# First-layer gate and value weights as scaled float16 pairs in blocks 0 and 1

## The chip, the cores and the metric

The kernel runs on one core of a Trainium2 chip. The metric is the device time of one execution in microseconds (us). The engines are named as the profile names them: PE (TensorE, the matrix engine; PEld is its weight load), DVE (VectorE), ACT (ScalarE), POOL (GpSimd) and SP (SyncE, which issues nearly all DMAs, in order).

## The reference

```python
# attention: q, k, v are (4, 8, 576, 64); tau = 0.02
scores = 0.125 * q @ k.T
scores = where(scores >= max(scores) - tau, scores, -1e9)
attn = exp(scores - max); attn = attn / (sum(attn) + 1e-9);  a = attn @ v
x = a as (2304 tokens, 512)
# layer 0: w_gate, w_val (512, 1536), w_out (1536, 512)
xn = x / sqrt(mean(x*x) + 1e-6) * rms_g
g = xn @ w_gate;  y = (g * sigmoid(g) * (xn @ w_val)) @ w_out
# layer 1: the same without the norm, with weights of its own
g = y @ w_gate2;  out = (g * sigmoid(g) * (y @ w_val2)) @ w_out2
```

All arrays are float32. The kernel reaches nearly that accuracy with products of split operands: each operand is a pair (high part, rest), and a product is three matmuls (high x high, high x rest, rest x high), written `for a, b_ in ((0, 0), (0, 1), (1, 0))`.

## The kernel before

The 2304 tokens are cut into three **blocks** of 768 (`NB`, `TW`; half a block is `HT` = 384 columns). A layer over a block is 18 **units** of weights (`NU`): 12 gate-and-value units (`gate_val`, 128 columns of gate and 128 of value each; the list `GV`) and 6 output units (`outp`). Units are numbered through: 0 to 17 are block 0, layer 0; 18 to 35 block 0, layer 1; 36 to 53 block 1, layer 0; 54 to 71 block 1, layer 1; 72 to 107 block 2. A unit before 54 is 48 matmuls of 384 columns (`dense`): per 128 columns of weights four slices, three products, two halves. From unit 55 on, gate-and-value units use seven products in place of eight (`gate_val7`, `weights7`); in block 2 these run on scaled float16 pairs, elsewhere on `float32r`, the type of all products of units 0 to 53.

Attention is cut into 48 tiles per block. Those of block 0 run first, alone; those of block 1 are interleaved with block 0's units, those of block 2 with block 1's layer 0. The first two units (`NRAW`) are computed on `x * rms_g` without the token's norm (`put_raw`) and scaled afterwards; then `norm(0)` writes the normed block into `XS`, the split input of a layer. At the end of a layer's `outp(2)`, `put` writes the next layer's `XS`.

**Weights.** In block 0, each unit is loaded as 1 MB of 64-bit words and turned to float32 by three ACT steps and one of DVE (L1006 to L1009, into one of two `w32` buffers); `w_split` (L968, L970) then makes the pair: ACT copies to `float32r`, DVE (for units in the set `W_E`) or POOL subtracts. The pair lies in one of three buffers (`r_w`) and is stored to DRAM for block 1 (`kept`, 1 MB); gate-and-value units also store the float32 weights (`kept2`, 0.5 MB). Units in the set `K_E` store the float32 weights alone, and are split again in block 1. In block 1, layer 1, `square_sum` (L863, L864) reads each of layer 0's gate-and-value units back and sums its squares; `power` turns the sums to scales, powers of two, for block 2's float16 pairs. The sum for `rms_g` is spread by a matmul inside `rms(1)` (L820).

**Order.** All operations are collected with priorities (`SU`, `ST` and the offsets `OFFS`) and put into an order by a list scheduler in the file (`Program.order`), which uses costs given with each operation. Each engine then runs its instructions in that order. The sets `V_E`, `Q_E`, `X_E`, `P_E`, `T_E`, `H_E` and others choose the engine of single operations.

Of the kernel before, what the change touches and what calls it, by code (L numbers as in the profile page):

```python
# [88 lines left out]

V_E = {1, 3, 6, 7, 8, 12, 14, 15, 16, 21, 24, 27, 28, 29, 30, 31, 32, 33, 35, 36, 37, 38, 39, 40, 43, 44, 46, 47, 48, 51, 53, 55, 56, 58, 59, 61, 63, 64, 66, 67, 68, 82, 83, 87, 90, 91, 95, 96, 97, 98, 100, 101, 102, 103, 106, 107, 109, 112, 116, 117, 122, 124, 125, 127}  # L90
K_E = {1, 3, 6, 7, 8, 12, 14, 18, 19, 20, 22, 24, 25, 26, 30, 31, 32, 33, 34}
W_E = {1, 2, 3, 6, 8, 11, 12, 13, 14, 16, 17, 18, 19, 21, 25, 27, 29, 30, 31, 33, 34, 37, 40, 41, 42, 44, 46, 49, 50, 51, 52, 55, 56, 57, 58, 59, 61, 62, 63, 64, 69, 72, 73, 74, 75, 78, 81, 82, 83, 85, 87, 89, 92, 93, 94, 96, 98, 99, 100, 102, 103, 106, 108, 110, 111, 113, 114, 117, 120, 121, 122, 125, 131, 133, 137, 138, 139, 141, 143}
H_E = {0, 1, 2, 4, 5, 8, 9, 11, 12, 14, 15, 18, 20, 21, 22, 23, 25, 27, 28, 32, 33, 34, 35, 36, 37, 40, 41, 44, 45, 46, 47, 48, 49, 51, 54, 55, 56, 57, 58, 59, 60, 61, 64, 65, 68, 69, 73, 74, 80, 84, 85, 87, 88, 93, 94, 95}
X_E = {0, 2, 4, 6, 8, 12, 17, 21, 22, 25, 28, 32, 33, 34, 35, 40, 41, 42, 43, 44, 47, 48, 50, 51, 55, 57, 58, 59, 62, 63, 64, 66, 74, 77, 80, 81, 82, 83, 85, 86, 87, 88, 89, 90, 91, 92, 93, 94, 96, 98, 99}
P_E = {0, 1, 2, 3, 4, 6, 7, 10, 12, 13, 14, 15, 16, 17, 18, 19, 22, 23, 25, 28, 29, 30}
# [1323 lines left out]
```

## Time and profile before

| | us |
|---|---|
| median of 3 runs | 1143.38 (1142.97 to 1148.64) |
| profiled execution | 1145.37 |
| its span, first to last instruction | 1143.5 |
| PE busy / DVE / ACT / POOL | 1108.9 / 908.4 / 792.1 / 613.5 |

A busy PE is not a PE at its peak: a matmul's bar is longer than the distance to the next one. The speed of PE is read from the distance of starts inside a run of matmuls. The trace shows attention of block 0 up to about 131 us, the units of block 0 to about 500 us, block 1's layer 0 to about 718 us, its layer 1 to about 872 us, and block 2 to the end.

### The profile page before, as it was taken

Reading aid. Unit: us, or ns where it says so; the run is one execution under the profiler, and the core shown is the slowest. Engines: PE = TensorE matmul, PEld = TensorE weight load, DVE = VectorE, ACT = ScalarE, POOL = GpSimd, SP = SyncE. Lnnn points to the kernel's source line nnn. Section 1 sums busy time; section 2 is a strip of 40 time slices with the busy share of each in tenths; the row PEclk is TensorE's granted clock in tenths of the full one; section 3 lists DMA queues with packets and bytes.
Section 4 is the critical chain, followed back from the end, with each engine's and each line's share of the span. In section 5 each row is a group of like instructions: output and inputs, shape, how many; then the busy total and the mean of one; then the engine's idle time right before and its main releaser. Section 6 shows DMA issues by size and latency. Waiting matters only on the chain.

```text
span 1143.5 us, 19688 instructions
## 1 busy us (share of the span) xinstructions
PE 1108.9 (97%) x7106; PEld 966.6 (85%) x7106; DVE 908.4 (79%) x1642; ACT 792.1 (69%) x1175; POOL 613.5 (54%) x818
## 2 busy tenths in 40 slices
PE   8989999999999999999999999999999999999998
PEld 5656889989999999998999998999997768668677
DVE  7989598988987888887888897876479767896844
ACT  5798689878889887645866555756675766776621
POOL 5476146765678887448798874143501264224501
PEclk8999999999999999999999999999999999999999
DMA  6564349999899999957788786733755232223011
GB/s 173 182 212 154 102 144 270 269 266 309 235 260 244 262 245 251 271 159 195 164 187 181 185 187 158 256 101 133 258 181 180 72 118 92 64 104 111 19 38 56
DMA packets 178898, 201.44 MB, mean 176 GB/s; under 512 B 144368, under 2 KB 148208, under 8 KB 168816
## 3 DMA queue, kind: packets, MB, share of 16 engines
q1 hardware_dynamic: 178512, 200.18, 61.7%
q8 instruction: 56, 0.92, 0.3%
q14 instruction: 42, 0.34, 0.1%
q10 hardware_dynamic: 288, 0.00, 0.0%
HBM read 135.66 MB, written 36.18 MB: 150 GB/s over the span
## 4 chain that ended last, share of the span: by engine, by line
PE 59%; DVE 14%; DMA 10%; ACT 6%; POOL 6%; issue 4%; SPq 0%; ACTq 0%; POOLq 0%; DVEq 0%
PE ps L1076 19%; PE pt L1113 7%; PE pbPA L1113 6%; PE pbPD L1076 5%; PE pbPB L1076 5%; DMA w<-kept 4%; DMA arena<-arena 4%; PE pt L1076 3%; PE ps L719 2%; PE pt L772 2%; PE pt L675 2%; PE ps L615 2%; PE pt L654 1%; POOL arena L578 1%; ACT w L864 1%
## 5 line engine op out<-in xcount | busy, mean ns | idle before, releaser
L1076 PE MATMUL ps<-XS,w 128*128 128x384 f32 x1152 | 210.5, 339 | 3.0 <-DVE th L1195 1.4
L1076 PEld LDWEIGHTS ps<-XS,w 128*128 128x128 f32 x1152 | 199.6, 189 | 5.1 <-DVE th L1195 1.7
L1113 PEld LDWEIGHTS <-arena 128*128 128x128 f16 x1008 | 97.2, 98 | 66.7 <-issue 4.1
L1076 PE MATMUL pt<-XS,w 128*128 128x384 f32 x600 | 111.0, 337 | 3.3 <-DVE th L1179 3.0
L1076 PE MATMUL ps<-h,w 128*128 128x384 f32 x576 | 106.9, 341 | 1.7 <-DVE col L734 0.7
L1076 PEld LDWEIGHTS pt<-XS,w 128*128 128x128 f32 x600 | 102.9, 188 | 5.7 <-DVE th L1179 4.6
L1047 POOL TENSOR_TENSOR arena<-w,arena 128x384 f16<-128x384 f32 (+3 forms) x52 | 62.3, 1223 | 81.9 <-ACT arena L1045 74.5
L1076 PEld LDWEIGHTS ps<-h,w 128*128 128x128 f32 x576 | 101.4, 190 | 3.5 <-issue 1.7
L1218 POOL TENSOR_TENSOR h<-th,h 128x384 fp32r<-128x384 f32 (+1 forms) x35 | 55.3, 1592 | 91.1 <-ACT h L1214 91.0
L735 ACT ACTIVATE arena<-ps,col 128x576 f32<-128x576 f32 x96 | 70.5, 737 | 38.4 <-DVE col L734 20.6
L733 DVE TENSOR_REDUCE col<-ps 128x1 f32<-128x576 f32 x96 | 71.4, 751 | 27.0 <-PE ps L719 26.8
L736 DVE SCALAR_TENSOR_TENSOR arena<-ps,col,arena 128x576 f32<-128x576 f32 x96 | 77.5, 810 | 13.8 <-ACT arena L735 13.4
L1214 ACT CAST h<-th 128x768 fp32r<-128x768 f32 x72 | 60.0, 833 | 38.9 <-DVE th L1176 14.1
L1113 PE MATMUL pt<-rx,arena 128*128 128x384 f16 (+1 forms) x384 | 82.8, 330 | 0.8 <-ACT tq L1122 0.8
L1076 PE MATMUL pbPB<-h,w 128*128 128x384 f32 x420 | 82.2, 340 | 1.3 <-DVE h L1218 1.3
L1076 PE MATMUL pbPD<-h,w 128*128 128x384 f32 x420 | 80.8, 339 | 1.4 <-DVE h L1218 0.8
L1113 PE MATMUL pbPA<-rx,arena 128*128 128x384 f16 (+1 forms) x368 | 78.8, 330 | 2.8 <-ACT SS L1122 1.9
L578 POOL TENSOR_TENSOR arena<-arena 128x512 f16<-128x512 f32 x68 | 81.0, 1193 | 0.1
L1076 PEld LDWEIGHTS pbPD<-h,w 128*128 128x128 f32 x420 | 73.7, 188 | 2.5 <-DVE h L1218 1.2
L1076 PEld LDWEIGHTS pbPB<-h,w 128*128 128x128 f32 x420 | 73.9, 188 | 2.3 <-DVE h L1218 1.6
L559 ACT ACTIVATE arena<-arena,col 128x576 f32<-128x576 f32 x76 | 65.0, 864 | 14.6 <-DVE col L746 8.9
L1042 DVE TENSOR_TENSOR w<-w 128x256 f32<-128x256 f32 x108 | 58.1, 554 | 20.9 <-DMA w<-kept 11.5
(275 smaller groups left out, 2696.9 us busy)
## 6 DMA issues: line engine op xcount, KB each, us to landing
w<-kept SPq DMA_DIRECT2D x77, 512.0 KB, 4.0
w<-in_w SPq DMA_DIRECT2D x36, 1024.0 KB, 6.8
w<-kept SPq DMA_DIRECT2D x25, 1024.0 KB, 5.5
kept<-w SPq DMA_DIRECT2D x17, 1024.0 KB, 4.8
kept<-w SPq DMA_DIRECT2D x26, 512.0 KB, 4.1
arena<-in_qkv SPq DMA_DIRECT2D x40, 160.0 KB, 4.2
ra<-in_qkv SPq DMA_DIRECT2D x10, 576.0 KB, 4.7
out<-Y SPq DMA_DIRECT2D x11, 384.0 KB, 2.9
```

The costliest lines, as they stand in the source:

```text
L559: op("ACT", 760, lambda: nc.scalar.activation(e, e, AF.Identity, bias=c[:, 4:5], scale=c[:, 3:4]), **k)
L578: op(en, 601 if eng == 2 else 1128, lambda: n1.tensor_tensor(h[:, 640:], e[:, :512], h[:, :512], ALU.subtract), lock=True, w=[("lo", n)], ...
L615: nc.tensor.matmul(s[m:m + w, jj, :b - a], x[k, c0:c0 + w], x[k, S + a:S + b], start=True, stop=True)
L733: op("DVE", 670, lambda: nc.vector.tensor_reduce(c[:, 0:1], s2, AX.XY, ALU.max, negate=True), w=[*sk, ("mx", n)], bufs=[cb], p=T + F['MAX' ...
L735: op("ACT", 640, lambda: nc.scalar.activation(e2, s2, AF.Exp, bias=c[:, 2:3], scale=SCALE), r=[("thr", n)], w=[*sk, ("e", n)] + ek, bufs=[ ...
L736: op("DVE", 750, lambda: nc.vector.scalar_tensor_tensor(e2, s2, c[:, 1:2], e2, ALU.is_ge, ALU.mult, accum_out=c[:, 6:7]), r=[("thr", n)], ...
L1042: op(en, 345 if en == "DVE" else 740, lambda n1=n1, o=o, x=x, y=y, alu=alu: n1.tensor_tensor(q(o), q(x), q(y), alu), lock=True, w=[("w32", ...
L1047: op(en, 70 + (z - a) * 105 // 100 if en == "DVE" else 190 + (z - a) * 210 // 100, lambda a=a, z=z: n2.tensor_tensor(hv(1)[:, a:z], st[:, ...
L1076: nc.tensor.matmul(pt[:, j, :HT] if len(halves) == 2 else pt(), w(i, a), x(i, b_)[:, j * HT:(j + 1) * HT], start=(i == 0 and a == 0 and b_ ...
L1113: nc.tensor.matmul(bank(), w()[:, a, col * 256 + i * P:][:, :P], xf(i, b_), start=first and i == 0 and a == 0 and b_ == 0, stop=i == 1 and ...
L1214: op("ACT", 734, lambda: nc.scalar.copy(h[:, 0], tb.t), r=[("th", n)], w=[("h0", n)], bufs=[tb, hb], p=p, name=f"h{n}")
L1218: op(eng, 72 + (z - a) * 105 // 100 if eng == "DVE" else 190 + (z - a) * 209 // 100, lambda a=a, z=z: n1.tensor_tensor(h[:, 1, a:z], tb.t[ ...
```

## The change

Layer 0's gate-and-value units of blocks 0 and 1, but for units 0 and 1, become scaled float16 pairs, and so does their input `XS`. Units 0 and 1 stay `float32r` in block 0; their twins 36 and 37 are float16. The scales are made in block 0: after a unit's conversion, ACT sums its squares, PE spreads the sum over the partitions, and six small DVE operations make the scales; ACT and DVE then make the pair (`split16`). Tanh and value operations take the scales as operands. The pair is stored (`keptg`, 0.5 MB) with the float32 weights (`kept2`, 0.5 MB), and block 1 loads the pair as it is; units 36 and 37 are split from float32. `K_E` keeps only layer 1's units. `square_sum` in block 1, layer 1, goes. The three weight buffers become `A`, `B` and a third that is either one `float32r` buffer (`C`) or two of float16 (`D`, `E`): layer 0's float16 units take turns on D and E, its other units on A and B, layer 1's on C, A, B. `XS` changes its type with each layer (`GEN`), so a `put` waits for all reads of the old `XS`. All offsets and most of the engine sets have other values.

```diff
-K_E = {1, 3, 6, 7, 8, 12, 14, 18, 19, 20, 22, 24, 25, 26, 30, 31, 32, 33, 34}
+K_E = {18, 19, 20, 22, 24, 25, 26, 30, 31, 32, 33, 34}
...
+    GEN = (1, 2, 3, 4, 5, 5)
...
-    r_w = ring("w", 3, [P, 2, 1024], F32R)
+    WT = [sb.tile([P, 2, 1024], F32R, name=f"w{i}") for i in range(2)]
+    late["wc", 1] = sb.tile([P, 2048], F32, name="wc_3", tag="wc")
...
+    def half16(n):
+        return n < SB0 and n % (2 * NU) in GV[:NF] and n >= NRAW
+
+    def w_next(n):
+        layer = n // NU
+        g = min(layer, 3) + 1
+        cycle = "DE" if half16(n) else ("AB", "CAB")[layer % 2 or layer > 3]
...
-            if b == 1:
-                nc.tensor.matmul(bank(pk)[:, 400:401], ones[:, 0:1].to_broadcast([P, P]), SETS16[0][0][:, 12:13], start=True, stop=True)
...
+    def col_sum(x, r, p):
+        op("PE", 100, lambda: nc.tensor.matmul(PA[:, 1, 400:401], ones[:, 0:1].to_broadcast([P, P]), x, start=True, stop=True), r=r, w=["SCB"], p=p, name="scales", cols=0)
...
     def norm(b):
-        T = SU(36 * b) - 3000 + 0
+        T = SU(36 * b) - 3000 + (NP0, NP1, NP2)[b]
         last = b == NB - 1
+        xsb.ops = old()
...
-        if gen == 1:
+        if gen:
             bufs = bufs + [Buf(None, xsb)]
...
+    def split16(n, k, w, ws, b32, sbf, p):
+        sc = SETS16[0][2][:, k:k + 1]
+        op("ACT", 939, lambda: nc.scalar.activation(ws()[:, 0], w, AF.Copy, scale=sc), ...)
+        op("DVE", 1142, lambda: nc.vector.scalar_tensor_tensor(ws()[:, 1], w, sc, ws()[:, 0], ALU.mult, ALU.subtract), ...)
...
+            if half16(n):
+                if i in K_E or i < NRAW:
+                    op("DMA", 1500, lambda: nc.sync.dma_start(w, kept[i][:, 0] if i in K_E else kept2[i]), ...)
+                    split16(n, GV.index(i), w, ws, b32, sbf, T + O(n)['WS2'])
+                else:
+                    op("DMA", 1500, lambda: nc.sync.dma_start(ws(), keptg[i]), ...)
+                return
...
-        w_split(n, w, ws, b32, sbf, T + O(n)['WS'])
+        if n < NU and n in GV:
+            k = GV.index(n)
+            op("ACT", 1100, lambda: nc.scalar.activation(t.bitcast(BF16)[:, :1024], w, AF.Square, accum_out=SETS16[0][0][:, k:k + 1]), ..., name=f"wsq{n}")
+            col_sum(SETS16[0][0][:, k:k + 1], [("SSQ", 0, n)], T + O(n)['WS'] + O(n)['WR'])
+            power(0, lambda: (PA[:, 1, 400:401], 1.0), ["SCB"], k, k + 1, ...)
+            unit_scales(0, T + O(n)['WS'] + O(n)['WR'], k, k + 1)
+        if half16(n):
+            split16(n, GV.index(n), w, ws, b32, sbf, T + O(n)['WS'])
+        else:
+            w_split(n, w, ws, b32, sbf, T + O(n)['WS'])
...
+        elif n < NU and n in GV:
+            if half16(n):
+                op("DMA", 1500, lambda: nc.sync.dma_start(keptg[n], ws()), ..., name=f"keep{n}")
+            op("DMA", 1500, lambda: nc.sync.dma_start(kept2[n], w), ..., name=f"keep{n}")
...
-                dense(pt, pk, NC, ..., lambda i, a: XSF()[:, a, i], wk, xk, [wb], T, U)
+                dense(pt, pk, NC, ..., lambda i, a: XSF(xg)[:, a, i], wk, xk, [wb], T, U, ns=165 if h16 else 175)
...
-                if b == 1 and m == 1:
-                    square_sum(GV[f], SETS16[0][0][:, f:f + 1], ("SSQ", 0), T)
-                    if f == NF - 1:
-                        weight_scales(0, T)
-                        unit_scales(0, T)
```

## Rows read from the trace of the kernel before

**Rows 1.** Page, busy time: engine, us, share of the span, instructions.
```profile
PE 1108.9 (97%) x7106; PEld 966.6 (85%) x7106; DVE 908.4 (79%) x1642; ACT 792.1 (69%) x1175; POOL 613.5 (54%) x818
```
**Rows 2.** Stages: PE, PEld, DVE, ACT, POOL busy us (instructions), clock, DMA share, GB/s.
```profile
150.00:310.00 160.00, 156.87 (x938) 149.57 (x937) 139.51 (x223) 134.20 (x164) 102.84 (x121) 1.00 0.93 261
310.00:486.00 176.00, 173.70 (x1056) 162.50 (x1056) 148.41 (x240) 144.07 (x177) 131.83 (x155) 1.00 0.97 254
502.00:718.00 216.00, 211.21 (x1417) 198.08 (x1416) 177.66 (x392) 135.02 (x228) 165.02 (x254) 1.00 0.76 179
718.00:872.00 154.00, 149.18 (x849) 145.51 (x848) 112.28 (x186) 99.91 (x163) 48.51 (x39) 1.00 0.53 183
872.00:1143.50 271.50, 265.91 (x1587) 198.13 (x1585) 197.79 (x312) 159.97 (x241) 84.75 (x78) 1.00 0.23 81
```
**Rows 3.** PE's waits in 150 to 310 us: us in total, times, longest.
```profile
PE ps L1076 <- DVE th L1195: 1.6, 2, 1.4
PE ps L719 <- DVE arena L736: 0.9, 1, 0.9
```
**Rows 4.** Timeline of PE, float32r runs: start, us, line, tile, shapes, count.
```profile
263.50 8.48 PE L1076 MATMUL ps<-XS,w 128*128 128x384 f32 x48
...
293.60 7.59 PE L1076 MATMUL ps<-h,w 128*128 128x384 f32 x42
```
**Rows 5.** Timeline of PE, float16 runs of block 2.
```profile
894.66 1.14 PE L1113 MATMUL pt<-rx,arena 128*128 128x384 f16 x6
895.64 1.14 PE L1113 MATMUL pbPA<-rx,arena 128*128 128x384 f16 x6
```
**Rows 6.** Timeline of PE, one-column and two-column matmuls.
```profile
129.12 1.50 PE L818 MATMUL pt<-small,SS 128*128 128x2 f32 x12
...
485.91 0.36 PE L820 MATMUL pt<-sqs,small 128*128 128x1 f32 x2
```
**Rows 7.** Timeline of DVE, first and last of four dependent scale operations.
```profile
487.87 0.15 DVE L869 TENSOR_SCALAR sqs<-pt 128x1 f32<-128x1 f32 x1
...
488.49 0.14 DVE L872 TENSOR_SCALAR sqs<-sqs 128x1 int32<-128x1 int32 x1
```
**Rows 8.** The sums of squares: ns min/median/max, first and last start us.
```profile
L864 ACT ACTIVATE w<-w x30: 1040/1057/1074, 656.0 to 843.6; 128x1024 bf16<-128x1024 f32 x30
L864 ACT ACTIVATION_READ_ACCUMULATOR w<-w x30: 185/186/206, 657.0 to 844.5; 128x1 f32 x30
```
**Rows 9.** Groups by shape, pair's rest: busy us, mean ns, idle before.
```profile
L970 DVE TENSOR_TENSOR w<-w,w 128x1024 fp32r<-128x1024 f32 x28 | 42.4, 1516 | 4.7 <-ACT w L968 4.6
L1047 DVE TENSOR_TENSOR arena<-w,arena 128x1024 f16<-128x1024 f32 x15 | 20.3, 1353 | 0.0
```
**Rows 10.** Stage 500 to 718 us: busy us (count) of ACT at L968.
```profile
500.00:718.00 218.00, 8.37 (x8) 1.00 0.76 178
```
**Rows 11.** Timeline around the switch from unit 1 to unit 2, all engines.
```profile
141.27 4.67 PE L1076 MATMUL ps<-XS,w 128*128 128x384 f32 x26
...
144.02 3.02 ACT L952 CAST XS<-X 128x768 fp32r<-128x768 f32 x4
...
145.81 3.55 DVE L955 TENSOR_TENSOR XS<-X,XS 128x768 fp32r<-128x768 f32 x4
...
146.81 4.43 PE L1076 MATMUL ps<-XS,w 128*128 128x384 f32 x24 [0.87 <-DVE XS L955]
```
**Rows 12.** Timeline, all engines: unit 8's pair is made, and PE behind it.
```profile
189.12 1.05 ACT L968 CAST w<-w 128x1024 fp32r<-128x1024 f32 x1 [0.67 <-DVE w L1009]
...
193.77 1.22 DVE L970 TENSOR_TENSOR w<-w,w 128x1024 fp32r<-128x1024 f32 x1
...
203.57 6.41 PE L1076 MATMUL ps<-XS,w 128*128 128x384 f32 x36
```
**Rows 13.** Page, DMA issues: count, KB each, median us to landing.
```profile
w<-kept SPq DMA_DIRECT2D x77, 512.0 KB, 4.0
...
w<-kept SPq DMA_DIRECT2D x25, 1024.0 KB, 5.5
```

More of the change, by code (lines that the diff above doesn't have):

```diff
@@ L903, in y_scale, with old @@
             op("ACT", 734, lambda o=o: nc.scalar.activation(Y[:, o], Y[:, o], AF.Copy, scale=SETS16[1][2][:, 12:13]), r=[("SC", 1, 12)], w=[("Y", o)], p=p + 1000 * o, name="y_scale")
+    def old():
+        keys = [(f"XS{a}", c) for a in (0, 1) for c in range(NC)]
+        return list({pg.wrote[k] for k in keys} | {i for k in keys for i in pg.read.get(k, ())})
     def norm(b):
-        T = SU(36 * b) - 3000 + 0
+        T = SU(36 * b) - 3000 + (NP0, NP1, NP2)[b]
         last = b == NB - 1
+        xsb.ops = old()
         for c in range(NC):
-            put(c, X[:, c], [("Xn", b, c)] + XK(c, 0, TW), [xbuf] if last else [], T, ("POOL", "DVE")[8 * b + c in P_E], HT if last and c < 2 else TW, int(last))
+            put(c, X[:, c], [("Xn", b, c)] + XK(c, 0, TW), [xbuf] if last else [], T, ("POOL", "DVE")[8 * b + c in P_E], HT if last and c < 2 else TW, GEN[2 * b])
         if last:
@@ L1153, in gate_val @@
                 n = u[0]
-                ahead(n + 2)
+                ahead(n + 1 if half16(n + 2) else n + 2)
                 cur_unit[0] = n
@@ L1262, in outp @@
                             if m == 0:
-                                put(o, Y[:, o], [("Y", o)], [], T + U + O(n)['DR'] + O(n)['PUT'], ("POOL", "DVE")[8 * b + 4 + o in P_E], HT if o < 2 and b > 1 else TW, int(b > 1))
+                                put(o, Y[:, o], [("Y", o)], [], T + U + O(n)['DR'] + O(n)['PUT'], ("POOL", "DVE")[8 * b + 4 + o in P_E], HT if o < 2 and b > 1 else TW, GEN[2 * b + 1])
                             else:
@@ L1331, in body @@
     op("ACT", 60, lambda: nc.scalar.dma_start(rgs, rg), w=["rg"], p=-1e9, name="rg")
+    op("ACT", 200, lambda: nc.scalar.activation(SETS16[0][3][:, :4], rgs, AF.Square, scale=32.0, accum_out=SETS16[0][0][:, 12:13]), r=["rg"], w=["sqx", ("CA", 0)], p=20000, name="sqx")
+    col_sum(SETS16[0][0][:, 12:13], ["sqx"], 20000)
+    power(0, lambda: (PA[:, 1, 400:401], 1.0), ["SCB"], 12, 13, 20000)
+    op("DVE", 75, lambda: nc.vector.tensor_scalar(rgx, rgs, SETS16[0][2][:, 12:13], 1.0, ALU.mult, ALU.mult), lock=True, w=[("SC", 0, 12)], p=20000, name="scales")
     done = [0]
```

139 lines of the change are left out of this document (83 added, 56 removed), and 8 rows, old and new, of the table OFFS.

## The prediction

> **What bounds the kernel now.** I read the page's busy times first, then busy time by stage, then PE's waits, then the timelines for the distance between matmuls. PE is busy for 97% of the span [rows 1]; the stages show that this is so in each of them from 150 us to the end: PE idles 3.1 us of the 160 us from 150 to 310 us (block 0, layer 0, with attention tiles of block 1), 4.8 us of 216 in block 1's layer 0, and 4.8 us of 154 in block 1's layer 1, and the clock is 1.00, the full 2.4 GHz, in all five [rows 2]. PE's waits in the first of these stages are two late DVE results, 1.4 us at worst [rows 3]. So the time follows PE's work there. What makes it delicate are the neighbours: from 150 to 310 us DVE is busy for 87%, ACT for 84%, and the DMA engines for 93% [rows 2].
>
> **PE's work.** In a float32r run, 48 matmuls of 384 columns take 8.48 us; less one matmul's own 0.34 us (the last one's bar) that is 47 distances of 173.2 ns; the 42 matmuls of the other run give 41 of 176.8 ns [rows 4]. Two float16 runs of six start 0.975 us apart, 162.5 ns per matmul of the same width [rows 5]. The change turns 10 units of block 0 and 12 of block 1 to float16, 22 x 48 = 1056 matmuls. At 10.7 ns that is 11.3 us, at 14.3 ns 15.1 us; I take 12, nearer the long run, since most runs are uncut: 5.5 in block 0, 6.5 in block 1.
>
> The gap formula of the Trainium skill (TensorE: Matmul & The Clock Gate, Back-to-back issue gap) makes the distance columns / 2.4 + 2.5 ns, without regard to the type: 162.5 ns for float16 and float32r alike. The float16 runs agree to the nanosecond, the float32r runs lie 11 to 14 ns above it [rows 4, 5]; by the rule alone the 12 us would be nothing, and the sum 12 us higher. The trace decides against it, but it is a rival below.
>
> **The new sums on PE.** Twelve spreading matmuls come in, each two records if they go like the one in `rms(1)`: that pair takes 0.36 us by itself, and in a run of twelve such records the distance is (1.50 - 0.29) / 11 = 0.11 us [rows 6]. About three (units 0 to 2, converted early) fall into attention alone, where PE has room. Nine at 0.22 to 0.36 us are 2.0 to 3.2 us; below, they could fall into gaps and cost nothing. I take 2.4 and give back 0.4 for the spreads that go in `rms(1)` and in block 1's layer 1: +2.0. A spreading matmul also waits for ACT's sum, and behind it in PE's order stand products that need nothing from it. The order puts it where it is due by its own costs, so most of these waits should be short; no row shows one. From 0 to the longest wait of rows 3 for all nine, that is 0 to 12.6 us; I take 1.0, near the low end, because PE's two kinds of wait in the stage add up to 2.5 us although every product there has such a release.
>
> **ACT and DVE in block 0.** Each of the 12 sums of squares is 1.06 + 0.19 = 1.24 us of ACT [rows 8], 14.9 us together; it moves from block 1's layer 1. Some eight units (6 to 9, 12 to 15) are converted between 150 and 310 us: +9.9 us on 134.2. The six scale operations depend on each other; four such in `rms(1)` start 0.21 us apart [rows 7], so six are 1.24 us, on eight units 9.9 us of DVE. The pair's rest is now always DVE's: three units that were POOL's (7, 9, 15) add 3 x 1.35 us, and the float16 form is 0.16 us cheaper than the float32r one on the other units [rows 9], some -0.8. The new engine sets give POOL part of DVE's splits of the attention input for the first heads of block 1 (`V_E` loses six of its entries below 48), which I put at about -4. DVE comes to 139.5 + 9.9 + 4.1 - 0.8 - 4 = 149 and ACT to 144 us, of a stage that should shrink to some 158: 94% and 91%. That fits, and attention tiles can move into layer 1, where DVE and ACT stand at 84% and 82% of 176 us [rows 2]. If the cover were gone altogether, the stage would be as long as DVE's extra work, about 10 us more. I charge queueing with half of the 3.1 us that PE idles in the stage now: +1.7.
>
> **The switch of `XS`.** Today ACT starts the new high parts at 144.02 us while unit 1's last products still run until 145.94, because chunk 0 has been read; DVE's first rest follows at 145.81, and PE starts unit 2 at 146.81 after 0.87 us of idling [rows 11]. With another type in the same memory, all chunks wait for 145.94. From there one high part (0.83 us, the 3.02 us cover four with overlap) and one rest (0.95) and two hand-overs of about 0.25 give 148.2: +1.4 us; bounds 0 (other products of PE stand there) and 3.0 (ACT's four high parts first). The later switches have `outp(2)`, 96 matmuls or 16.6 us at 173 ns, between the last read and the first need, and cost nothing; without that cover each would cost the same 1.4.
>
> **Two float16 buffers in place of a ring of three.** Unit 8's pair was made from 189.12 to 195.0 us and first read inside the run that starts at 203.57 [rows 12], at least 8.6 us early. With D and E, its making waits for unit 6's products, and unit 7's 48 matmuls, 7.8 us at 162.5 ns, lie between that and the need. The making itself is 1.05 us on ACT and 1.35 on DVE [rows 9, 12], so 5.4 us are left for queueing: 0. In block 1 the wait is a load: 512 KB land in 4.0 us, against 5.5 us for 1 MB [rows 13], again inside 7.8 us. SP is in order: a load that waits for D or E holds the attention transposes queued behind it. I cost that at nothing as long as those transposes land an attention tile ahead; if they don't, it is the first wait to look for.
>
> **What goes.** In block 1's layer 0 seven units are split again today, two will be. ACT's eight copies from 500 to 718 us take 8.37 us, 1.05 each [rows 10]: -5.2 us of ACT, with the rests on DVE and POOL, and 8.5 MB of loads become 6. In layer 1, 14.9 us of ACT and twelve loads of 512 KB go. These engines aren't the bound there, and PE idles only 4.8 us in each of the two stages [rows 2]: worth 0 to 9.6 us, I take 1.5. Stores in block 0 stay at 11 MB for these units (seven of 0.5 and five of 1.5 MB; ten of 1.0 and two of 0.5): 0, at a DMA share of 93%.
>
> **Sum.** -12.0 + 2.0 + 1.0 + 1.7 + 1.4 - 1.5 = -7.4 us. The profiled execution took 1145.4 us, 1.9 of it outside the span of 1143.5; changed it would be 1138.0. The median of the runs shown is 2.0 lower, 1143.4, and gives **1136 us**.
>
> **Rivals.** Within 0.5% (5.7 us) no change could be told from none; faster means below 1137.7, slower above 1149.1.
>
> - *As forecast*, 1136 (own range 1131 to 1140): chance 0.50.
> - *Block 0 keeps its length.* With DMA at 93%, DVE at 94% and ACT at 91%, the 5.5 us that PE saves there turn into waits for weights or attention, and only block 1 gains: 1136 + 5.5 = 1141.5. For it: three engines over 90% in one stage; against it: layer 1 has room on DVE and ACT (but none on DMA, 97%). Chance 0.23.
> - *Slower: the pairs of block 0 come late.* A pair now needs conversion, ACT's sum, a place in PE's order, six DVE steps, ACT and DVE again, and its buffer only one unit ahead. From a lateness of 0.9 us on each of the eight units the gain is gone; above 1.6 us the kernel is slower by more than 0.5%; at 2.0 us it is 1136 + 16 = 1152. For it: seven hand-overs between engines at over 90%; against it: the 5.4 us left, and that sum and scales can be made before the buffer is free. Chance 0.14.
> - *The relief in block 1 counts in full*, half of PE's 9.6 idle us there beyond my 1.5, and 15.1 instead of 12 us by the distance: 1136 - 3.3 - 3.1 = 1130. Chance 0.09.
> - *The distance does not fall* (by the page's formula above float32r had nothing to lose): 1136 + 12 = 1148. The rows of block 2 speak against it, where float16 runs at 162.5. Chance 0.04.
>
> The **range** from 1128 to 1149 leaves out most of the slower case and a tail of the fast one, under 0.2 together. Faster: 0.44 of the forecast's 0.50, the 0.09, and a little of block 0's case, 0.56. Slower: most of the 0.14 and a part of the last, 0.15. The rest, 0.29, is no change.
>
> **What would show it.** In the changed profile the float16 runs at the line of `dense` should stand 162 to 163 ns apart in 1056 matmuls; sums of squares should lie before 310 us and none in block 1's layer 1; PE should idle some 2 us before unit 2; the stage of block 1's layer 0 should be 6 to 8 us shorter, that of block 0's layer 0 about level to 2 us shorter. Wrong would be: PE's waits from 150 to 310 us above 8 us, with the pairs of `split16` or the spreading matmuls as releasers; a DMA that ends PE's waits in block 0; or float16 runs at 173 ns.

## The result: slower by 0.9%, where 0.6% faster was forecast

The changed kernel takes 1153.7 us (median of 6 runs, 1151.4 to 1156.3) against 1142.9 for the kernel before on the same chip (6 runs): ratio 1.0090 [1.0064, 1.0116]. The forecast was 1136 us in a range from 1128 to 1149. The profiled execution took 1153.4 us, its span is 1151.5, 8.0 over that of before.

The page of the changed kernel, busy times in the order of [rows 1]; PE's busy time fell by 3.5 us, DVE's rose by 7.9:
```profile
PE 1105.4 (96%) x7128; PEld 893.8 (78%) x7128; DVE 916.3 (80%) x1689; ACT 789.8 (69%) x1167; POOL 620.2 (54%) x836
```
Its stages, columns as in [rows 2]:
```profile
150.00:310.00 160.00, 149.16 (x910) 107.92 (x909) 134.28 (x268) 130.01 (x167) 87.23 (x116) 0.99 0.78 214
310.00:486.00 176.00, 174.37 (x1052) 165.71 (x1051) 154.45 (x240) 144.15 (x175) 135.78 (x155) 1.00 0.94 257
502.00:718.00 216.00, 210.79 (x1445) 160.23 (x1445) 185.11 (x416) 134.23 (x221) 147.78 (x238) 0.99 0.76 174
718.00:872.00 154.00, 148.78 (x845) 147.28 (x844) 113.97 (x173) 93.64 (x147) 49.43 (x43) 0.99 0.41 141
```
Only the first row is bad: from 150 to 310 us PE is busy for 149.2 us instead of 156.9. These rows are cut at fixed times, though, in which the changed kernel is some 10 to 20 us behind. Cut at the same products, from unit 2 to block 0's layer 1, the stage reads as follows, first in the kernel before and then in the changed one:
```profile
145.40:309.00 163.60, 159.60 (x953) 151.98 (x952) 143.11 (x228) 137.80 (x169) 101.84 (x121) 1.00 0.90 253
...
156.80:326.00 169.20, 160.24 (x975) 118.94 (x974) 143.41 (x279) 137.56 (x175) 101.18 (x129) 0.99 0.84 232
```
The stage is 5.6 us longer. PE idles for 9.0 us of it instead of 4.0, while DVE and ACT are as busy as before: 143.4 and 137.6 us, 85% and 81% of the stage. No engine became the bound there by its work; they wait for one another. PE's waits from 150 to 310 us are 11.0 us in place of 3.2, of which [rows 3] shows 2.5 (another 0.7 stood behind DVE's `Y`):
```profile
PE ps L743 <- DVE arena L760: 5.8, 6, 2.2
PE ps L1128 <- ACT xs L976: 2.4, 1, 2.4
PE ps L1128 <- DVE xs L979: 1.4, 2, 1.0
PE ps L1128 <- DVE th L1252: 0.8, 1, 0.8
PE ps L1128 <- DVE wc L996: 0.4, 1, 0.4
```
PE waits for a pair's rest (L996) once, 0.4 us. The long waits are attention's `QK` (L743, the product that makes its scores) behind DVE's mask (L760), and unit 2's input behind the switch of `XS` (L976, L979).

The float16 itself does what it should. The changed kernel's timeline of PE has a run of 42 in float16 and, in layer 1, one in float32r (start and duration first):
```profile
221.64 7.10 PE L1128 MATMUL ps<-xs,wc 128*128 128x384 f16 x42
...
343.12 7.44 PE L1128 MATMUL ps<-xs,w 128*128 128x384 f32 x42
```
Its weight loads take about half of float32r's (page, groups: busy us and mean ns of one behind the first bar):
```profile
L1128 PEld LDWEIGHTS <-wc 128*128 128x128 f16 x1056 | 100.3, 99 | 75.1 <-issue 10.5
...
L1128 PEld LDWEIGHTS ps<-h,w 128*128 128x128 f32 x576 | 100.1, 188 | 1.0 <-POOL h L1276 0.5
```
Where the time goes shows when the products are laid side by side: start of a product in the profiled execution of before, and how much later (us) it starts in the others. All kernels are those of the experiments below; "without sums" is the changed kernel without its sums of squares and scale steps. (Unit 2's first two products need high parts alone; they stand in the first run of [rows 11], ahead of the wait there.)

| | before | changed | without sums | float16, no scales | two buffers | scaled, order of before |
|---|---|---|---|---|---|---|
| unit 0 | 114.0 | +3.0 | +0.9 | -1.5 | -0.6 | +6.1 |
| unit 2 | 145.4 | +11.4 | +9.6 | -0.2 | +0.6 | +8.1 |
| unit 12 | 250.5 | +13.0 | +6.8 | -1.9 | +3.4 | +18.4 |
| block 0, layer 1 | 309.0 | +17.0 | +10.3 | -3.8 | +4.3 | +27.8 |
| block 1 | 501.3 | +13.3 | +6.9 | -5.1 | +3.5 | +27.4 |
| block 1, layer 1 | 723.0 | +8.4 | +1.3 | -7.5 | +12.7 | +22.0 |
| end of the span | 1143.5 | +8.0 | +3.5 | -7.0 | +8.9 | +22.8 |

The change loses 17 us up to the end of block 0's layer 0 and gets 9 back later.

**The first loss, 100 to 157 us.** The changed kernel's timeline, attention's end to unit 2 (start, us, engine, line; in brackets the idle time before and what ended it):
```profile
133.12 1.50 PE L842 MATMUL pt<-small,SS 128*128 128x2 f32 x12
...
135.93 0.17 DVE L852 TENSOR_SCALAR small<-small 128x6 int32<-128x6 int32 x1
...
138.05 1.13 ACT L1046 ACTIVATE w<-w 128x1024 bf16<-128x1024 bf16 x1 [3.49 <-DMA ra<-in_qkv]
...
138.60 0.72 POOL L568 TENSOR_TENSOR arena<-arena 128x320 f32<-128x320 f32 x1 [7.39 <-DMA arena<-in_qkv]
...
139.36 0.49 DVE L568 TENSOR_TENSOR arena<-arena 128x320 bf16<-128x320 f32 x1 [3.25 <-POOL arena L568]
...
139.76 0.16 DVE L855 TENSOR_TENSOR small<-small 128x6 f32<-128x6 f32 x1
...
142.43 2.25 PE L1128 MATMUL ps<-XS,w 128*128 128x384 f32 x6 [3.20 <-ACT Y L1248]
...
146.71 0.80 ACT L871 COPY SS<-ps 128x768 f32<-128x768 f32 x1 [2.68 <-PE ps L865]
...
155.95 2.29 ACT L976 CAST xs<-X 128x768 f16<-128x768 f32 x3
...
156.82 0.48 PE L1128 MATMUL ps<-xs,wc 128*128 128x384 f16 x2 [2.35 <-ACT xs L976]
```
`rms(0)` begins 4.0 us later than in [rows 6]. Its chain of small DVE steps, which run 0.2 us apart, stands still from 135.93 to 139.76, because a split of attention's next head (L568) is ahead of them in DVE's order and waits for POOL, which waits for a load. PE itself waits for something else there: 3.20 us at 142.43 for ACT's copy (L1248) that empties a bank, a part of the memory that PE writes to. That copy stands in ACT's order behind the conversion of a later unit's weights (L1046), which waited 3.49 us for a load. So unit 1's products end at 154.47, where their run in [rows 11] ends at 145.94: that is 8.5 of the 11.4 us. The high parts start at 155.95 instead of 144.02 [rows 11].

The table tells where this loss belongs. From unit 0 to unit 2 the changed kernel loses 8.4 us and the kernel without sums 8.7, but the three kernels in the order of before lose 1.2 to 2.0, with two buffers or with scales. So it belongs to the change's own order and engine sets, rather than to the scales or the buffers.

**The second loss, 250 to 270 us.** The timeline of the changed kernel at unit 13's scale, with unit 12's rest at the end:
```profile
255.55 1.06 ACT L1053 ACTIVATE w<-w 128x1024 bf16<-128x1024 f32 x1
...
257.38 0.35 PE L894 MATMUL ps<-sqs,small 128*128 128x1 f32 x2
...
259.93 0.16 DVE L885 TENSOR_SCALAR sqs<-ps 128x1 f32<-128x1 f32 x1 [1.94 <-ACT arena L759]
...
261.95 0.14 DVE L887 TENSOR_SCALAR sqs<-sqs 128x1 int32<-128x1 int32 x1
...
262.13 1.15 ACT L995 ACTIVATE wc<-w,sqs 128x1024 f16<-128x1024 f32 x1 [2.24 <-DVE sqs L887]
...
262.89 0.79 PE L743 MATMUL ps<-rx 128*128 128x288 f32 x4 [1.84 <-DVE arena L760]
...
263.41 1.27 DVE L996 SCALAR_TENSOR_TENSOR wc<-w,sqs,wc 128x1024 f16<-128x1024 f32 x1
```
From the sum to the high part pass 6.6 us; the three scale steps up to it were charged 0.2 us each, but lie among DVE's other work from 259.93 to 262.09. Unit 12's rest comes at 263.41 although its high part was done at 257.74, and attention's mask, which frees `QK`'s bank, queues in the same order. PE idles 1.84 us here and 2.21 us at 268.42, and then the granted clock falls (the last but two of the columns; in [rows 2] it is 1.00):
```profile
262.00:274.00 12.00, 8.51 (x41) 4.79 (x42) 8.98 (x25) 7.77 (x10) 7.81 (x11) 0.86 0.65 198
...
268.80:272.20 3.40, 3.40 (x14) 1.74 (x13) 2.02 (x6) 2.12 (x3) 3.07 (x5) 0.50 1.03 348
```

**The granted clock.** At 0.50 it is 1.2 GHz. From 130 us on, the profiled changed kernel has five such stretches of 3.4 us (from 135.7, 142.5, 268.8, 524.8 and 845.6 us), the kernel before two (from 132.0 and 487.0). The last four of the five begin within 1.5 us after a wait of PE of 2.2 to 3.3 us. A stretch at half the clock can cost at most half its length, so the three more are worth at most some 5 us of the 8.0. Over all runs the mean granted clock is 0.982 to 0.993 in the changed kernel and 0.990 to 0.999 in the kernel before. No run holds the clock fixed, so its part is not shown. An estimate: among the runs of one kernel 0.001 less clock goes with some 0.3 us more (126 runs of the changed kernel and the experiments), and the two means differ by 0.008, which would be 2 to 3 us. The clock follows PE's waits here, and it is not the whole loss: the scaled kernel in the order of before loses 24 us at a mean of 0.9915.

### The profile page after: what moved, and what is told of

It is laid out like the page before. It is cut to its first block, busy times and chain, and to the rows that moved or that the text cites. A ratio compares the mean times of both kernels' runs of the same rounds, so it can differ in the third digit from the quotient of the medians.

```text
span 1151.5 us, 19769 instructions
## 1 busy us (share of the span) xinstructions
PE 1105.4 (96%) x7128; PEld 893.8 (78%) x7128; DVE 916.3 (80%) x1689; ACT 789.8 (69%) x1167; POOL 620.2 (54%) x836
## 4 chain that ended last, share of the span: by engine, by line
PE 65%; DVE 14%; DMA 8%; ACT 7%; issue 3%; POOL 3%; SPq 0%; ACTq 0%; POOLq 0%; DVEq 0%
PE ps L1128 19%; PE pt L1166 8%; PE pbPA L1166 7%; PE pt L1128 6%; PE pbPD L1128 5%; PE pbPB L1128 5%; DMA w<-kept 4%; PE ps L743 3%; PE pt L699 2%; PE pt L796 2%; DMA arena<-arena 2%; DVE col L757 1%; PE ps L639 1%; PE pbPB L1166 1%; DMA arena<-in_qkv 1%
## 5 line engine op out<-in xcount | busy, mean ns | idle before, releaser
L1128 PEld LDWEIGHTS <-wc 128*128 128x128 f16 x1056 | 100.3, 99 | 75.1 <-issue 10.5
L1128 PE MATMUL ps<-xs,wc 128*128 128x384 f16 (+1 forms) x768 | 135.5, 332 | 5.3 <-ACT xs L976 2.4
L1128 PE MATMUL pt<-xs,wc 128*128 128x384 f16 (+1 forms) x600 | 105.7, 329 | 0.5 <-DVE th L1235 0.2
L760 DVE SCALAR_TENSOR_TENSOR arena<-ps,col,arena 128x576 f32<-128x576 f32 x96 | 77.5, 811 | 12.5 <-ACT arena L759 11.8
L1094 POOL TENSOR_TENSOR w<-w 128x256 f32<-128x256 f32 x60 | 51.3, 877 | 67.0 <-ACT w L1092 60.9
L743 PE MATMUL ps<-rx 128*128 128x288 f32 x416 | 76.8, 312 | 10.9 <-DVE arena L760 6.9
L743 PEld LDWEIGHTS ps<-rx 128*128 128x128 f32 x416 | 62.2, 190 | 19.8 <-DVE arena L760 9.6
L1272 ACT CAST h<-th 128x768 fp32r<-128x768 f32 x72 | 59.7, 829 | 23.6 <-DVE th L1200 11.4
L1276 POOL TENSOR_TENSOR h<-th,h 128x768 fp32r<-128x768 f32 (+1 forms) x35 | 59.3, 1698 | 22.9 <-ACT h L1272 22.9
L1097 ACT CAST arena<-w 128x768 f16<-128x768 f32 (+1 forms) x70 | 63.2, 939 | 1.1 <-DVE w L1094 1.0
L766 POOL TENSOR_SCALAR col<-col 128x1 f32<-128x1 f32 x96 | 34.9, 364 | 52.0 <-DVE arena L760 43.7
L1094 DVE TENSOR_TENSOR w<-w 128x256 f32<-128x256 f32 x80 | 46.7, 606 | 13.1 <-ACT w L1092 7.5
```

What stands on the lines that cost most here:

```text
L743: nc.tensor.matmul(s[:, j, :HS], x[:, c:c + P], x[:, k:k + HS], start=i + u == 0, stop=i == 1 and u == len(heads) - 1)
L760: op("DVE", 750, lambda: nc.vector.scalar_tensor_tensor(e2, s2, c[:, 1:2], e2, ALU.is_ge, ALU.mult, accum_out=c[:, 6:7]), r=[("thr", n)], ...
L1094: op(en, 345 if en == "DVE" else 740, lambda n1=n1, o=o, x=x, y=y, alu=alu: n1.tensor_tensor(q(o), q(x), q(y), alu), lock=True, w=[("w32", ...
L1097: op("ACT", 939 - 206 * late, lambda a=a, z=z: nc.scalar.copy(hv(0)[:, a:z], st[:, a:z]), r=[("w32", n)], w=[("wh", n, late)], bufs=[stb, ...
L1128: nc.tensor.matmul(pt[:, j, :HT] if len(halves) == 2 else pt(), w(i, a), x(i, b_)[:, j * HT:(j + 1) * HT], start=(i == 0 and a == 0 and b_ ...
L1272: op("ACT", 734, lambda: nc.scalar.copy(h[:, 0], tb.t), r=[("th", n)], w=[("h0", n)], bufs=[tb, hb], p=p, name=f"h{n}")
```

## The experiments

Each ran beside the kernel before on the same chip; ratios are to it, and a difference of ratios is turned to us with 1144. Runs of one kernel lie up to 6 us from their median, so only ratios with their intervals count. The difference of two ratios is good to 3 or 4 us, and positions in one profiled execution to some 1.5 us.

**1. The float16 distance alone.** The order of before, 22 units' operands read as float16:
```diff
+as16 = n < SB0 and n % (2 * NU) in GV[:NF] and n >= NRAW
+wv = lambda a, z: w[:, a, z:z + P].bitcast(F16)[:, :P] if as16 else w[:, a, z:z + P]
+xv = lambda i, a: XSF()[:, a, i].bitcast(F16) if as16 else XSF()[:, a, i]
```


> The kernel before, in its own order, with one thing changed: the 1056 products of layer 0's gate-and-value units (blocks 0 and 1, without units 0 and 1) read their two operands as float16 views of the same buffers. No weights are scaled, no sums, no other buffers; the numbers in these products are therefore meaningless. Theory A (PE's work sets the time, and the saving of 11 to 12 us is real but was eaten by what the change adds): 10 to 13 us faster than before, 1130 to 1133. Theory B (other engines hold the order back, so a faster PE gives little in any case): less than 5 us faster, above 1138.

1138.3 us, 0.9955 [0.9937, 0.9972]: 5.1 us for 12 saved on PE, at the edge of theory B. So the distance does fall, and it is worth less than half of what I charged. With block 1's units alone (`2 * NU <= n`):

> The order of before with float16 views in block 1's 12 units only (values without meaning), to be laid beside the run with all 22 units (5.7 us under before). Theory A (block 0 is held by the other engines, so its half of the saved PE time is worth next to nothing; block 1's is kept): 4 to 6 us under before. Theory B (each half is kept to about one half): 2.5 to 3.5 us under before.

1141.6 us, 0.9983 [0.9968, 0.9997]: 1.9 us, less than either theory has it, though the interval (0.3 to 4.1 us) reaches into B's 2.5 to 3.5. In its trace PE is 1.3 us ahead of before at unit 0 and 2.9 at block 1's first product, where no float16 has run yet (1.8 us of it come from 479 to 491 us, where before has its stretch at 1.2 GHz). It is 3.8 ahead at block 1's third unit and loses 3.4 of that by 615 us: a transpose by DMA is late, ACT waits for it, DVE for ACT, and PE, which waits 0.3 us from 585 to 630 in the kernel before, for DVE:
```profile
604.87 0.67 ACT L570 CAST arena<-arena 128x576 f16<-128x576 f32 x1 [3.78 <-DMA arena<-arena]
...
605.96 0.55 DVE L1182 SCALAR_TENSOR_TENSOR th<-th,pt 128x384 f32<-128x384 f32 x1 [2.84 <-ACT th L1181]
...
606.57 3.05 PE L1076 MATMUL pt<-XS,w 128*128 128x384 f16 x12 [2.11 <-DVE th L1182]
```

**2. The reads that go.** The order of before without the 12 reads and sums in block 1's layer 1 (constants in their place):
```diff
+gone = n < NU and n in GV
-op("DMA", 1500, lambda: nc.sync.dma_start(b32.t, kept2[n] ...
+op("DMA", 1500, (lambda: None) if gone else lambda: ...
```


> The kernel before in its own order without the twelve reads and sums of layer 0's squares in block 1's layer 1 (the scales come from a constant). It measures what the change gains there by itself. As predicted: 0.5 us faster, at most 3. If this relief were what the changed kernel should have gained and did not: more than 3 us faster.

1141.7 us, 0.9981 [0.9964, 0.9998]: 2.2 us, against 1.5 charged for this and for block 1's splits together.

**3. The sums.** The changed kernel with the sums of squares, spreading matmuls and scale steps not issued, and each half alone (`lambda: None` at these operations, the rest of the order untouched):

> The changed kernel in the changed kernel's order, with the twelve sums of squares, their twelve spreading matmuls and the 72 small DVE operations of block 0 not issued; the scales are constants set at the start, so the pairs are unscaled. Theory A1 (the chain of sums delays the pairs and the attention before them; it makes the stall of 7.6 us at 250 to 300 us and part of the late start): 8 to 12 us faster than the changed kernel, 1142 to 1146. Theory A2 (the loss is the switch of XS and in-order waits around 131 to 157 us, and the sums lie in gaps): under 4 us faster, above 1149.

> The changed kernel with only ACT's 12 sums of squares issued (their results unused; no spreading matmuls, no scale steps, constant scales): between the run without any of the sums (1146.25, 7.5 under the changed kernel) and the changed kernel. Theory A1 (ACT's 15 us are the price): 1150 to 1153. Theory A2 (the chain over PE and DVE is the price): 1146 to 1148.

> The changed kernel without ACT's 12 sums, with the spreading matmuls and the 72 scale steps issued on constant sums: the other half. Theory A1 (ACT's 15 us are the price): 1146 to 1148.5. Theory A2 (the chain over PE and DVE is the price): 1151 to 1153.

Without any 1146.3 us, 1.0014 [0.9995, 1.0033]; ACT's sums alone 1149.9, 1.0042 [1.0027, 1.0058]; the chain alone 1151.6, 1.0053 [1.0033, 1.0074]; all of it 1.0090. So the whole costs 8.7 us, as theory A1 of the first text has it (8 to 12 us). By halves, ACT's 15 us cost 3.2 us and the chain 4.5: they add up within the intervals, and neither is *the* price. As alternatives, A1 and A2 of the two other texts were both wrong.

**4. In-order waits at the start.** The changed kernel with DVE's split of head 18 behind `rms(0)`'s steps, and conversion 5 behind ACT's copy of unit 0's values:
```diff
+behind([("DVE", "split_v18")], ("DVE", "rms_rstd0"))
+behind([("ACT", "conv5"), ("DVE", "conv5")], ("ACT", "v0"))
```


> The changed kernel with two moves in its order, nothing else: DVE's split of the value input of head 18, which waited 3.25 us for a late DMA in front of the norm's steps, comes behind these steps; ACT's and DVE's conversion of unit 5, for whose load ACT waited 3.49 us in front of the copy that frees PE, comes behind the copies of unit 0. Theory A2 (in-order waits for late DMAs in front of the first units make the loss between 131 and 157 us): 3 to 5 us faster than the changed kernel, 1148 to 1151. Theory A1 (sums): within 1.5 us of it.

1156.9 us, 1.0127 [1.0109, 1.0145], slower. The steps now run through to 136.77, but the next operation in DVE's order is another one that waits, and the last step comes at 146.08 instead of 143.11:
```profile
142.60 1.23 DVE L1049 SCALAR_TENSOR_TENSOR w<-w,t 128x1024 uint32<-128x1024 uint32 x1 [5.66 <-ACT t L1048]
143.74 2.30 DVE L856 SCALAR_TENSOR_TENSOR small<-small 128x6 f32<-128x6 f32 x1
```
PE's longest wait from 125 to 180 us is now for that last step:
```profile
PE ps L865 <- DVE small L857: 7.1, 1, 7.1
```
One wait was moved and the next one in the queue took its place.

**5. The switch of `XS`.** The changed kernel with block 0's `XS` left in the float32r buffer and read as float16, and ACT's high parts right behind unit 1's products; then the same without the sums:
```diff
+g = gen if gen > 1 else 0
+hi, lo = [lambda a=a: XSF(g)[:, a, c] for a in (0, 1)]
+seq = rest[:z] + picked + rest[z:]      # picked: ACT's put0 to put3 of block 0, z: behind mm1
```


> The changed kernel with block 0's XS kept in the float32r buffer and read through float16 views (values of block 0 without meaning), and ACT's four high parts placed right behind unit 1's last products in its order, so that unit 2's input follows chunk by chunk as in the kernel before. Theory A (the switch of XS is a main part of the 10 us that stay with the sums gone): 2.5 to 4 us under the changed kernel, ratio to before 1.0055 to 1.007. Theory B (the delay is already there before the switch, and what the switch adds is made up later or is lost to the next late pair): less than 1 us under it, ratio 1.008 to 1.010.

> The same, and with the 12 sums of squares, spreading matmuls and 72 scale steps not issued (constant scales). Theory A: the two add up, 1142 to 1144 us, 2.5 to 4 under the run without sums (1146.25). Theory B: within 1 us of the run without sums, 1145.3 to 1147; then the rest is in the order in which the changed kernel's work is written out.

1151.5 us, 1.0069 [1.0048, 1.0090], and without sums 1149.6, 1.0048 [1.0031, 1.0065], not under the run without sums alone (1.0014). The first is in theory A's range, but its gain of 2.4 us lies within the intervals; the second is over both theories and denies it. So what the switch costs in this order is unclear.

**6. Block 1 alone.** Block 0 in float32r, its sums of squares on ACT with nobody waiting, block 1's layer 0 in scaled float16, the order of before:
```diff
+nc.scalar.activation(r_t.slots[0].t.bitcast(BF16)[:, 1::2], w, AF.Square, accum_out=SETS16[0][0][:, k:k + 1])
+return 2 * NU <= n < 3 * NU and n - 2 * NU in GV      # the float16 units
```


> The kernel before with the change in block 1 alone, in the order of before: block 0 stays float32r without scales; the 12 sums of squares are made on ACT behind each unit's conversion in block 0 (nobody waits for them), their scales in rms(1) in the instructions that are there for X's; in block 1's layer 0 all 12 units are split as scaled float16 pairs from 512 KB loads. The 12 reads and sums in block 1's layer 1 and five 1 MB stores of block 0 go. Theory A (the loss lies in block 0: the scales' chain, the switch of XS and the order they force; block 1's part is worth what the chip showed of it, about 4 by the pitch and 2.4 by the reads): 5 to 8 us under the kernel before, 1136 to 1139, ratio 0.993 to 0.9955. Theory B (the pairs cost as much on DVE and ACT wherever they are made, and what PE saves turns into waits): within 3 us of before, 1141 to 1147.

1155.0 us, 1.0102 [1.0077, 1.0126]: neither theory. It is 5.4 us behind at block 1 (up to there only ACT's sums are new, and five stores are gone) and 10.4 behind at block 1's layer 1, where DVE makes the rests of 12 scaled pairs in place of seven splits shared with POOL. The sums here write every second place of a scratch buffer and take 1.38 us each on ACT instead of 1.06. The order of before, which has no place for the added work, charged it in both blocks.

**7. The float16 without scales.** The order, engines and ring of three of before; pairs and `XS` in float16 for the 22 units, the real switch, no scales in blocks 0 and 1 (constants for layer 0 in block 2):
```diff
+return NRAW <= n < SB0 and n % (2 * NU) in GV[:NF]    # half16
+op("ACT", 939, lambda: nc.scalar.copy(pair16(ws)[:, 0], w), ...
+op(en, ..., lambda: n1.tensor_tensor(pair16(ws)[:, 1], w, pair16(ws)[:, 0], ALU.subtract), ...
```


> The kernel before, in its order and on its engines, with the 22 units' pairs and XS in float16 in blocks 0 and 1 but without scales: no sums of squares, no scale steps, a ring of three buffers as before, POOL keeps its rests, real switch of XS between the types; the 12 reads in block 1's layer 1 go and layer 0's scales of block 2 are constants. What it leaves of the change is the float16 itself. Theory A (the loss is made by the sums, which put 15 us on ACT and a chain on DVE and PE into block 0, and by the order that they force): 5 to 8 us under before (5.7 by the pitch, 2.4 by the reads, a switch of 1.4 to 3 against), 1136 to 1139. Theory B (the retyped buffers themselves, the switch of XS and pairs in float16, cost what is left of the 10 us): within 3 us of before or above it, 1141 to 1148.

1136.5 us (1135.6 to 1138.4), 0.9930 [0.9912, 0.9948]: 8.0 us *faster than before* and some 18 under the change. Theory A holds. Its first stage, columns as in [rows 2]:
```profile
150.00:310.00 160.00, 154.26 (x948) 116.50 (x947) 142.46 (x225) 135.59 (x166) 104.63 (x124) 1.00 0.92 255
```
PE idles 5.7 us there, and the matmuls of a run of 48 in its timeline stand (7.98 - 0.33) / 47 = 162.8 ns apart:
```profile
260.94 7.98 PE L1116 MATMUL ps<-xs,w 128*128 128x384 f16 x48
```
With block 0's `XS` read in place, for the switch alone:

> The same with block 0's XS left in the float32r buffer and read through float16 views (values of block 0 without meaning), so that unit 2's input may follow chunk by chunk: what the switch of XS costs by itself. Theory A (the switch costs about what was charged): 1 to 3 us under the run with the real switch. Theory B (it costs nothing, since other products of PE stand there): within 1 us of it.

1138.8 us, 0.9947 [0.9930, 0.9963]. Neither theory: this kernel is not faster. From unit 0 to unit 2 the real switch loses 1.3 us (-1.5 to -0.2 in the table), the one in place 0.1; in the time of the kernel nothing of it is left. And with block 2's scales summed from the data as before:

> The float16 kernel without scales in blocks 0 and 1, but with the 12 reads and sums of squares left in block 1's layer 1, so that block 2's scales come from the data as in the kernel before. If the two gains add up (5.7 by the pitch, 2.4 by the reads), 5 to 7 us under before, ratio 0.994 to 0.9955; if the reads now stand in the way of more, since PE runs ahead, 2 to 4 us under it.

1137.7 us, 0.9946 [0.9929, 0.9964]: 6.2 us under before, so the gains of the distance and of the reads add up. Both kernels, this one and the first of this section, beat the kernel before and the changed one; what they give up is the scaling of layer 0's weights to a known size in float16.

**8. The rests and the buffers.** The same kernel with every rest on DVE in the change's form; with two pair buffers (`D`, `E` in one slot, writes moved behind their last reader); with both:
```diff
+lambda: nc.vector.scalar_tensor_tensor(pair16(ws)[:, 1], w, ones[:, 0:1], pair16(ws)[:, 0], ALU.mult, ALU.subtract)
+cycle = "DE" if half16(n) else ("AB", "CAB")[layer % 2 or layer > 3]
```


> The float16 kernel without scales, in the order of before, with the pairs made as in the change: ACT's copy with a scale operand (of ones) and every rest on DVE as one scalar_tensor_tensor, so that the six rests that POOL makes in blocks 0 and 1 come to DVE. Theory (a) (DVE's six rests more are a good part of the 10 us): 3 to 8 us over the same kernel with POOL's rests (1136.5), 1139.5 to 1144.5. Theory (c) (the order is the loss): within 2 us of it, 1135 to 1138.5.

> The float16 kernel without scales with the change's buffers: two halves of one buffer for the float16 pairs, the two others for the units between, and every write moved behind the last reader of its buffer in the order of before. Theory (b) (the two pair buffers are a good part of the 10 us): 3 to 8 us over the ring of three, 1139.5 to 1144.5. Theory (c): within 2 us of it, as the prediction had it (0 charged).

> Both at once. Theories (a) and (b): 1142 to 1147, the level of the changed kernel without its sums (1146.25). Theory (c): 1135 to 1140; then the remaining 6 us or more are in the order.

The rests: 1139.8 us, 0.9958 [0.9944, 0.9972], 3.2 us more for six rests that come to DVE (theory (a), at its lower end). Three of the six lie in block 1, where the change loads its pairs ready made, so this is no exact price of the change's own rests. Two buffers: 1157.5 us, 1.0133 [1.0109, 1.0157], 23 us more, far over what theory (b) gave; both: 1157.0, 1.0117 [1.0095, 1.0139]. PE's waits of the two-buffer kernel from 505 to 720 us (2.5 and 1.8 us with three buffers):
```profile
PE pt L1130 <- DVE th L1235: 10.3, 7, 4.1
PE pt L1130 <- DVE th L1232: 4.8, 3, 1.7
```
The longest of them in the timeline of PE:
```profile
540.24 5.74 PE L1130 MATMUL pt<-xs,w 128*128 128x384 f16 x24 [4.14 <-DVE th L1235]
```
PE doesn't wait for a pair there but for DVE, which empties a bank. SP's waits from 525 to 541 us show the way to it: a split's rest on POOL, which this order has behind the last reader of its buffer, holds the load that takes over its source:
```profile
SPq L1038 <- POOL w L1018: 5.8, 1, 5.8
```
In the timeline of all engines attention's transposes (L607) stand behind that load, and DVE idles 4.86 us for one of them, with PE's bank next in its order:
```profile
533.76 0.34 SPq L1038 DMA_DIRECT2D w<-kept  x1
...
534.16 1.93 SPq L607 DMA_TRANSPOSE arena<-arena  x1
...
539.27 0.46 DVE L595 CAST arena<-arena 128x576 f16<-128x576 f32 x1 [4.86 <-DMA arena<-arena]
539.64 0.55 DVE L1235 SCALAR_TENSOR_TENSOR th<-th,pt 128x384 f32<-128x384 f32 x1
```

**9. Scales with three buffers, and where a scale is read.** Next came the whole change with its scales in the order of before and a ring of three:
```diff
+a = add(t0, square, d)                                        # ACT's sum, ahead of the high part
+b = add(tp, lambda: nc.tensor.matmul(col, ones[:, 0:1]...     # next place on PE, 1.6 us later
+c = add(tp + 600, steps, [b])                                 # scale steps on DVE
```


> The whole change, with scales from the data (12 sums of squares, 13 spreading matmuls, scale steps, ACT and DVE making every pair with its scale), but with the ring of three buffers and the order of the kernel before: each sum stands on ACT ahead of its unit's high part, its spreading matmul at the next place on PE 1.6 us later, the scale steps behind it on DVE, and only what depends on them moves back. Theory A (the terms add: 1139.8 with the rests on DVE and 7.5 for the sums; two buffers and the order made for them cost the changed kernel the rest): 1145 to 1149, 5 to 9 us under the changed kernel. Theory B (the chain can't be had in an order that does not plan for it, so three buffers don't help): 1151 or more.

1168.0 us, 1.0207 [1.0184, 1.0230]: theory B. (Its sums take 1.35 us each on ACT, as in experiment 6.) All of it is lost in block 0 (table), by the same waits as in the changed kernel, only longer. PE's from 150 to 310 us:
```profile
PE ps L742 <- DVE arena L759: 13.8, 8, 2.5
```
DVE's there:
```profile
DVE sqs L1386 <- PE ps L742: 6.6, 3, 3.1
```
And one scale in the timeline of all engines:
```profile
264.89 0.38 PE L1382 MATMUL ps<-sqs,small 128*128 128x1 f32 x2
265.13 0.78 PE L742 MATMUL ps<-rx 128*128 128x288 f32 x4
...
265.95 0.16 DVE L1386 TENSOR_SCALAR sqs<-ps 128x1 f32<-128x1 f32 x1 [3.15 <-PE ps L742]
```
DVE stands idle for 3.15 us before the first scale step. Until 265.27 the spread sum itself (L1382) is not there; the last 0.6 us are for attention's scores (L742), which were written behind it. The mask is behind the scale step in DVE's order, and the next `QK` behind the mask. This kernel is 28 us over the one with the rests on DVE (0.9958); the changed kernel, with its own order and two buffers, is 15 over it.

A scale's first step reads the spread sum out of the bank of attention's scores, and so waits for what was written there after it. The next run tries whether this coupling is the price: in the changed kernel, this step stands right behind its spreading matmul:
```diff
+for j in [...]:                       # the spreading matmuls
+    seq.remove(j + 1)                 # the step that reads the sum
+    seq.insert(seq.index(j) + 1, j + 1)
```


> The changed kernel with the first scale step of every unit, which reads the spread sum out of the bank of attention's scores, right behind its spreading matmul in the order, ahead of the scores' next products, so that it waits for the spread alone and they for it. Theory A (the coupling of the scale steps to attention's tile through that bank is a good part of the chain's 4.5 us): 2 to 4 us under the changed kernel, ratio to before 1.0055 to 1.0073. Theory B (DVE has other work of the same length in its order, so the chain costs by its place in the queues): within 1.5 us of it, 1.0077 to 1.0103.

1154.1 us, 1.0076 [1.0053, 1.0098], between the two theories, and the interval takes in A's range and most of B's: undecided. A gain of 2 to 4 us on the changed kernel (1.0090 [1.0064, 1.0116]) is neither shown nor excluded. PE's waits from 150 to 310 us show the coupling turned around, scores behind scale steps:
```profile
PE ps L743 <- DVE arena L760: 3.9, 4, 1.8
...
PE ps L743 <- DVE sqs L885: 1.3, 4, 0.6
```

## Why the prediction was wrong, step by step

- *Distance, -12.0.* The distance was right: (7.10 - 0.33) / 41 = 165 ns in the changed kernel, 162.8 over 48 without scales. Its worth was not: 5.1 us. A PE that is busy for 97% of a stage is not thereby what bounds it; the order of DVE, ACT and the transposes can set the pace too, as the late transpose in experiment 1 shows. This is the reason behind the rival *block 0 keeps its length*. In the trace of experiment 1 block 0 kept most of it: PE is 1.4 us ahead at unit 0 and 3.3 at block 1, 1.9 for the 5.5 charged. Block 1 alone did no better, 1.9 us for 6.5. The gap formula of the Trainium skill (TensorE: Matmul & The Clock Gate, Back-to-back issue gap), weighed in the prediction, is given on that page for an isolated matmul and has no term for the type. The changed kernel's trace goes against it again: in its float32r run of 42 from 343.12 us the matmuls stand (7.44 - 0.34) / 41 = 173.2 ns apart.
- *Sums on PE +2.0, their waits +1.0, queueing +1.7.* This is the step that failed worst. Measured, the sums cost 8.7 us and the rests on DVE 3.2: 11.9 for 4.7. The spreads' own time was about as charged (0.33 us for each pair of records); what was wrong is the queueing. I compared DVE's and ACT's work with the stage's length and gave the scale steps 0.21 us each from a row where nothing stands between them [rows 7]. Cut at the same products, DVE and ACT did not even reach the 94% and 91% that were to fit, but 85% and 81%, and PE waited all the same. In the stage the steps lie up to a microsecond apart and block, or are blocked by, what is queued beside them. That the sums of the first units cost nothing in attention was wrong too: unit 0 starts 3.0 us late, 0.9 without the sums; which part of them does it is not told apart.
- *PE's waits in the stage.* They were read as two kinds, 2.5 us; the trace of before has a third row, 0.7 us behind DVE's `Y`. It changes little.
- *Switch of `XS`, +1.4.* Right in an order that suits it (+1.3 at unit 2); in the changed order 3.7 us of waits stand there instead of 0.87, behind products of unit 1 that end 8.5 us late already.
- *Two float16 buffers, 0.* Not nothing in an order written for three: 23 us, by the wait that the text named as the first to look for (transposes behind a load on SP) and then costed at nothing. The argument looked at one unit's 7.8 us of slack, not at what is queued behind a split that waits. How much of it the change's own order, which is written for two, still pays, no run shows.
- *Relief in block 1, -1.5, with -6.5 of the distance.* Two thirds of it came: from block 1's start to the end the changed kernel gains 5.3 us on before (+13.3 to +8.0), of 8.0 forecast. Experiments 1 and 2 give 1.9 for the distance and 2.2 for the reads.
- *Rivals.* "The pairs come late" had the sign and the chain, but its place was wrong: PE waits for a pair's rest 0.4 us in all. The lateness is passed on by DVE's and PE's queues to attention. As the text's own test had it, PE's waits exceed 8 us; their releasers are not the ones named.

Adding up in ratios: the forecast was -7.4 us and +10.3 came, 17.7 apart. The float16 without scales gives -8.0 where distance, switch and relief were to give -12.1: 4.1 of the 17.7. The sums and rests cost 11.9 for 4.7: another 7.2. The last 6.4 lie in the two buffers, in the order written around them and the scales, and in the engine sets. They were not told apart, since that order can't be had without them, and their cause stays open. The loss before unit 2 points to the order. Some 2 to 3 us of the whole may come by the granted clock, by the estimate above.

## What to carry to other kernels

In this kernel several engines are busy for 84% or more of a stage and each works through a fixed order. Added work cost a fifth to two fifths of its length there (ACT's 14.9 us cost 3.2; six rests of 1.3 us on DVE 3.2), and work saved on the busiest engine gave back less than half (5.1 us of 12; 1.9 of 6.5). Each of these is good to 2 or 3 us, so they are a first guess for another kernel and not a rule; but don't charge nothing because the sums fit. A value that must travel ACT, PE, DVE, ACT before work can go on costs its queues, not its instructions: twelve of them, with ACT's sums, cost 28 us in an order that did not plan for it. Before a buffer is taken from a ring, list what stands behind the instruction that will wait for it.

## What was not expected of the hardware

A float32r weight load takes 188 ns and a float16 one of the same shape 99 (rows of the page above), so the loads' busy time from unit 2 to block 0's layer 1 falls from 152.0 to 118.9 us. This agrees with the Trainium skill (TensorE: Matmul & The Clock Gate, Weight-path perf modes), which gives the fast load to types other than FP32. Whether that is why float32r matmuls stand 173 to 177 ns apart was not tried.
